# A new step list for a block-sparse attention and mixer kernel: engine order, load issues and PSUM banks

## The chip, the cores and the metric

The kernel runs on one core of a Trainium2 chip. The metric is the time of one execution on the device in microseconds (us); less is better. The time before is the median of 3 runs, 272.63 us (271.21 to 273.03).

## The reference, cut to what matters

Four batches, 8 heads, 768 positions, head size 64. Attention with a block mask (32 x 32 blocks: neighbours, the first and last block, and 3 sampled blocks for each block row), then a low-rank mix over the positions, then a two-layer network with a residual:

```python
scores = scale * np.matmul(q, k.transpose(0, 1, 3, 2))
scores = np.where(mask, scores, -1000000000.0)
attn = np.exp(scores - max); attn = attn / (sum + 1e-09)
x = np.matmul(attn, v)                      # heads side by side: (4, 768, 512)
u = x + (x.transpose(0, 2, 1) @ U @ V).transpose(0, 2, 1)      # rank 32
out = u + np.maximum(u @ w_ch1, 0.0) @ w_ch2                   # 512 -> 2048 -> 512
```

## The kernel before, in words

Tiles have 128 partitions. Heads are worked on in pairs, so there are 16 pairs, four to a batch: pairs 0 to 3 are batch 0, 4 to 7 batch 1, and so on. For each pair TensorE makes scores (keys by queries), ScalarE writes their exponential to the tile `est`, VectorE multiplies by the 0/1 `mask` (for pairs 0 to 3 the mask is added inside the score product instead, and no multiplication follows), and TensorE multiplies `est` with the values `vt`, with a column of ones for the row sums. VectorE then divides: `divide` (L538) is a reciprocal (L544) and one or two multiplications (L551). The mix goes through `Ut` and `Vt`; the result, transposed, is `uT`, for the products with the first weight `w1t` (`w1`, L679; matmuls L685) into PSUM, a rectifier into `hid` by ScalarE (L697) or VectorE (L699), and the products with the second weight `w2t` (`product`, L756, matmuls L760). The products with `w2t`, and for the last batch those with `w1t` too, are done as seven block products instead of eight (Strassen's scheme), which needs sums and differences of weight blocks (`weight_sum`, L723, VectorE, L721) and of token blocks.

PSUM has 8 banks. Every product is told its bank in the list; a product into a bank waits until the last reader of that bank is through.

The order is written out by hand: the string `PLAN` (L448) is a list of words, and a loop (L1141) issues each word's instructions to the engines in that order. Every engine works through its own instructions strictly in the order of the list and waits where an operand or a bank isn't ready; between engines only such waits order the work. So a word's place sets what stands ahead of it and behind it on its engine. The words that matter here:

- `S`, `B`: a score product of pairs 0 to 3, over one or two key tiles. `Q`: the scores of both heads of a pair over two key tiles (three `Q` make a pair; two `H` can stand for one `Q`). A digit is the bank.
- `e`: the exponential (ScalarE) of the oldest score product; `p`: the multiplication by the mask (VectorE), L1045.
- `A`, `V`: the products with the values; `v`: the division (VectorE) of the oldest finished one, two for each pair.
- `R`, `Z` without dots: transposes of q and k by TensorE; `t`, `z`: their copies out of PSUM (VectorE).
- `M`, `X`, `Y`, `E`, `m`, `y`, `g`: parts of the mix and their copies or sums.
- `P`, `C`, `U`: products with `w1t`; `P2` is the first half of one into bank 2, `P6` into bank 6; `a`, `b`: the rectifier on ScalarE or VectorE.
- `q.k.n`: weight sum k of half n. `S.`, `H.`, `D.`: sums, products and result sums of the down projection of batches 0 to 2; `g.`, `c.`, `o.`, `r.`, `s.`, `h.`, `e.`: the last batch.
- `F.`, `x.`, `d.`, `T.`: the mix at the end of a batch; `T.i` is the transpose of pair i's part to `uT` by a DMA (L623).
- `Z.b.tau.u`: a store of one row group of batch b (L707). `L.i`: loads: the DMA transposes of q and k of pair i + 2 (`front`, L386, SP queue) and the loads of pair i + 3 (GpSimd queue, L146).

The second weight comes in four loads on GpSimd's queue, each of four row tiles j of 16 (`load_w2`, L370), two of them among the loads of pair 7 and two among those of pair 8:

```python
for j in js:                                   # 0, 4, then 8, 12
    nc.gpsimd.dma_start(out=w2t[:, j : j + 4, :], in_=moe_w_ch2[j * P : (j + 4) * P, :]...)
```

A weight sum with k = 3 is `t1 = b12 - b11`, and for half n = 0 it reads row tiles 0 to 3 of `w2t`; k = 4 reads tiles 8 to 11 (n = 0) or 12 to 15 (n = 1):

```python
c, js = slice(n, n + 1), slice(n * NH // 2, (n + 1) * NH // 2)     # NH = 8
b11, b21 = w2t[:, 0:NH, 0:DM][:, js], w2t[:, NH:, 0:DM][:, js]
b12, b22 = w2t[:, 0:NH, DM:][:, js], w2t[:, NH:, DM:][:, js]
...
    3: (t1, b12, b11), 4: (t2, b22, t1), 5: (t4, b21, t2), ...
```

`t1` goes to the tile `res`, in which q and k of pairs 0 to 3 lay. It is an operand of product 5 of the down projection (`H.b.tau.5`).

Of the kernel before, what the change touches and what calls it, by code (L numbers as in the profile page):

```python
# [23 lines left out]
def kernel(  # L24
# [16 lines left out]
    B, H, S, D = q.shape  # L41
    BLK = 32
    NB = S // BLK
    T = S // P
# [404 lines left out]
    S0 S3 e e S5 B0 e Z7 e S3 z Z6 e z B0 A7 A e R6 S3 t A R5 e A B0 t A K6 e A S3 k v A5 A e K6 k B0 A  # L449
    A e K7 A K6 k S3 k A K7 e v B0 k S3 e M6 e A5 A m R7 A t B0 K6 R3 e k A A t S6 A e v S0 D2 S3 e d A7  # L450
    A e A S0 K6 A e S3 k K2 A e S5 k A e v S3 R2 e S5 t S0 e M7 e S3 m D2 e B5 d A0 D1 e A A d A S3 D2 A
    e d K1 S5 k R7 e S3 t A S1 e v A5 A e A S3 S6 e K2 A e A k A S3 v B0 e K7 M6 e k S3 m X5 K7 e A6 Y k
    A B0 y X7 Y e S3 y E5 A e A g A R7 S0 t A e v S4 S2 e A7 A e R1 E6 A t A g A A Q v e e M6 X7 m Y P6
    y p H U7 e p H b C e p H b U7 e p H b U6 e p E1 a g p V7 Q v e e V6 U7 v p U0 a P1 b C p P6 a C E7 Q
    a g U6 e e U7 b P6 b p U0 C a U7 p a Q b X6 Y e e P7 y C P6 b C p U0 b a p V7 L.5 Q v U.0.1.3.6 e
    q.3.0 V7 a.0.1.3.0 e U.0.1.1.1 v U.0.1.11.0 a.0.1.1.1 U.0.1.5.6 q.3.1 a.0.1.11.1 p Q a.0.1.5.1 p
    U.0.1.10.6 e U.0.1.7.7 a.0.1.10.0 e U.0.1.2.6 a.0.1.7.0 S.0.0.1.3 U.0.1.9.7 p a.0.1.2.1 Q a.0.1.9.1
    q.7.1 U.0.1.4.6 e S.0.0.2.0 H.0.0.1.0.7 p H.0.0.1.1 a.0.1.4.1 U.0.1.0.0 p L.6 e U.0.1.14.1 q.4.1 V6
    a.0.1.0.1 p a.0.1.14.1 Q v q.4.0 e V6 D.0.0.0 S.0.0.3 H.0.0.6.0 e v U.0.1.13.2 q.7.0 H.0.0.6.1
    U.0.1.12.6 a.0.1.13.1 D.0.0.2 y p Q a.0.1.12.1 q.5.1 H.0.0.7.0 e H.0.0.7.1 q.5.0 H.0.0.5.0.6 D.0.0.3  # L460
    H.0.0.5.1 e S.0.0.4.4 U.0.1.6.1 p H.0.0.4.0 a.0.1.6.1 H.0.0.4.1 D.0.0.4 Q D.0.0.5 p H.0.0.3.0 e L.7
    H.0.0.3.1 p H.0.0.2.0.7 H.0.0.2.1 e p U.0.1.8.2 U.0.1.15.0 D.0.0.1 D.0.0.6 a.0.1.8.1 V7 p a.0.1.15.1
    S.0.1.1.1 Q S.0.2.1.0 V6 e v S.0.1.2.4 H.0.1.1.0.7 y v H.0.1.1.1 y H.0.1.2.0.0 S.0.2.2.3 y H.0.1.2.1
    e D.0.1.0 M6 D.0.1.1 H.0.2.1.0.1 m H.0.2.1.1 S.0.2.3 F.1.0.2.4 D.0.2.0 F.1.1.3.6 F.1.2.5.0 x.6.0
    H.0.2.6.0 x.6.1 d.6.0 H.0.2.6.1 x.7.0 d.6.1 F.1.3.6.4 D.0.2.2 H.0.1.6.0 T.6 x.5.1 H.0.1.6.1 S.0.1.3
    H.0.2.7.0 H.0.2.7.1 x.4.0 H.0.2.5.0.6 x.5.0 H.0.2.2.0.0 D.0.2.3 d.5.0 H.0.2.2.1 x.4.1 d.5.1
    H.0.2.4.0 D.0.1.2 d.4.0 T.5 x.7.1 H.0.2.4.1 d.7.0 H.0.1.7.0 D.0.2.1 d.4.1 D.0.2.5 H.0.1.7.1 d.7.1
    S.0.2.4.2 T.4 Q D.0.1.3 H.0.2.5.1 e H.0.1.4.0 T.7 D.0.2.4 H.0.1.4.1 H.0.2.3.0 e D.0.1.5 H.0.2.3.1
    Z.0.0.1 p H.0.1.5.0.7 Z.0.2.1 H.0.1.5.1 D.0.2.6 Q Z.0.2.0 D.0.1.4 Z.0.0.0 S.0.1.4.0 U.1.0.0.6 e
    H.0.1.3.0 a.1.0.0.0 H.0.1.3.1 e U.1.0.11.6 D.0.1.6 p U.1.0.10.0 Z.0.1.0 Z.0.1.1 a.1.0.11.1 U.1.0.9.7  # L470
    p L.8 a.1.0.10.1 U.1.0.6.6 a.1.0.9.1 p Q a.1.0.6.1 p U.1.0.12.6 e V7 e U.1.0.2.2 v U.1.0.5.0 p
    a.1.0.12.1 U.1.0.1.7 a.1.0.5.1 a.1.0.2.1 U.1.0.3.6 a.1.0.1.0 p Q a.1.0.3.1 V6 p e U.1.0.4.7 v e
    U.1.1.5.2 a.1.0.4.0 U.1.0.15.6 p a.1.1.5.1 U.1.1.9.7 a.1.0.15.1 p Q a.1.1.9.1 U.1.1.3.7 e L.9
    U.1.0.7.6 a.1.1.3.0 e U.1.0.14.7 a.1.0.7.0 p U.1.1.4.0 U.1.1.10.6 a.1.0.14.1 a.1.1.4.0 U.1.1.1.7 p
    a.1.1.10.1 Q a.1.1.1.1 V7 e V6 v e U.1.1.7.7 v Q a.1.1.7.1 p U.1.0.8.7 e H.1.0.1.0.6 a.1.0.8.0
    H.1.0.1.1 p e U.1.1.13.7 p U.1.0.13.0 U.1.1.14.2 p a.1.0.13.1 a.1.1.13.1 U.1.1.8.3 S.1.0.1.3
    a.1.1.14.1 U.1.1.6.7 a.1.1.8.1 S.1.0.3 Q a.1.1.6.1 S.1.0.2.0 H.1.0.2.0.7 e D.1.0.0 L.10 H.1.0.2.1
    S.1.0.4.4 H.1.0.6.0 D.1.0.1 H.1.0.6.1 e U.1.1.15.1 U.1.1.11.0 a.1.1.15.0 U.1.1.0.7 p a.1.1.11.1 Q
    D.1.0.2 a.1.1.0.1 p y V7 e H.1.0.7.0 v e H.1.0.7.1 U.1.1.2.0 p U.1.1.12.7 D.1.0.3 a.1.1.2.1 p Q
    a.1.1.12.1 S.1.1.1.0 H.1.0.4.0 e H.1.0.4.1 S.1.1.2.1 V7 D.1.0.5 e S.1.1.3 H.1.1.1.0.6 p H.1.1.1.1 Q  # L480
    D.1.1.0 v H.1.1.6.0 e L.11 p H.1.1.6.1 H.1.0.5.0.7 D.1.1.2 H.1.0.5.1 e p H.1.1.7.0 H.1.1.7.1 D.1.0.4
    V0 y p y y H.1.1.5.0.3 S.1.1.4.3 y V4 y D.1.1.3 v H.1.1.5.1 v y H.1.1.4.0 H.1.1.4.1 S.1.2.1.1 y
    H.1.0.3.0 D.1.1.4 M4 S.1.2.2.0 H.1.0.3.1 m D.1.1.5 F.2.0.5.4 F.2.1.0.1 D.1.0.6 Z.1.1.1 H.1.2.1.0.6
    x.8.0 H.1.2.1.1 x.10.0 d.8.0 H.1.1.3.0 x.10.1 d.10.0 F.2.2.7.5 D.1.2.0 F.2.3.4.2 d.10.1 H.1.2.2.0.1
    x.8.1 T.10 H.1.2.2.1 x.11.0 H.1.1.3.1 x.9.0 d.11.0 H.1.2.6.0 x.11.1 d.8.1 H.1.2.6.1 d.9.0 D.1.1.6
    T.8 H.1.1.2.0.7 D.1.2.1 d.11.1 x.9.1 H.1.1.2.1 S.1.2.3 d.9.1 Q T.11 D.1.2.2 D.1.1.1 e H.1.2.7.0
    H.1.2.7.1 T.9 H.1.2.5.0.7 D.1.2.3 e H.1.2.5.1 S.1.2.4.2 H.1.2.4.0 Z.1.1.0 H.1.2.4.1 Z.1.0.1 Q
    D.1.2.5 D.1.2.4 U.2.0.4.6 p e H.1.2.3.0 a.2.0.4.0 H.1.2.3.1 e U.2.0.12.6 D.1.2.6 U.2.0.5.7 Z.1.2.0
    Z.1.0.0 a.2.0.12.1 Q Z.1.2.1 a.2.0.5.0 p U.2.0.2.7 e L.12 U.2.1.8.6 a.2.0.2.0 U.2.1.1.7 a.2.1.8.1 e
    U.2.0.11.2 a.2.1.1.0 U.2.0.15.6 p a.2.0.11.1 U.2.0.0.7 p Q a.2.0.0.1 p a.2.0.15.1 U.2.0.9.7 e V6  # L490
    a.2.0.9.0 p e U.2.0.8.0 v U.2.0.10.7 a.2.0.8.1 U.2.1.4.6 a.2.0.10.0 p Q a.2.1.4.1 V7 p e U.2.1.0.6 v
    e U.2.0.13.1 a.2.1.0.0 U.2.0.1.7 p a.2.0.13.1 U.2.1.2.6 a.2.0.1.1 p Q a.2.1.2.0 U.2.1.9.7 e L.13
    U.2.0.7.6 a.2.1.9.0 e U.2.0.6.7 a.2.0.7.0 p U.2.0.14.6 a.2.0.6.1 q.0.1 Q a.2.0.14.1 p V7 e q.0.0 V6
    v e q.1.1 U.2.0.3.7 v Q a.2.0.3.1 p H.2.0.1.0.7 e p U.2.1.5.6 H.2.0.1.1 S.2.0.1.4 e U.2.1.10.0
    a.2.1.5.0 U.2.1.14.1 S.2.0.2.1 a.2.1.10.0 U.2.1.3.6 a.2.1.14.1 D.2.0.0 Q S.2.0.3 a.2.1.3.1 p
    H.2.0.6.0 e H.2.0.2.0.6 p H.2.0.6.1 H.2.0.2.1 e D.2.0.2 U.2.1.13.0 D.2.0.1 S.2.0.4.3 H.2.0.7.0
    a.2.1.13.1 H.2.0.7.1 p y Q p V6 e D.2.0.3 H.2.0.4.0 v e H.2.0.4.1 V6 D.2.0.5 p Q v U.2.1.11.7 e
    H.2.0.5.0.6 a.2.1.11.0 H.2.0.5.1 q.1.0 e U.2.1.12.7 p U.2.1.15.0 p a.2.1.12.1 U.2.1.7.1 a.2.1.15.1
    U.2.1.6.7 p a.2.1.7.1 Q a.2.1.6.1 D.2.0.4 y S.2.1.1.4 Z.2.0.1 H.2.2.1.0.7 e H.2.2.1.1 S.2.1.3
    H.2.0.3.0 D.2.2.0 H.2.0.3.1 e p H.2.1.1.0.1 H.2.1.1.1 S.2.2.1.2 H.2.1.2.0.0 y V3 p y y S.2.1.2.3 y  # L500
    V4 v D.2.1.0 H.2.2.5.0.5 y v H.2.1.6.0 H.2.1.6.1 S.2.2.3 y H.2.1.2.1 S.2.2.2.1 M3 D.2.0.6 H.2.2.5.1
    m Z.2.0.0 D.2.1.2 F.3.0.6.3 F.3.1.4.2 x.12.0 H.2.2.6.0 x.12.1 H.2.2.6.1 d.12.0 H.2.1.7.0 x.14.0
    d.12.1 H.2.1.7.1 x.14.1 d.14.0 T.12 D.2.2.2 F.3.2.4.6 d.14.1 F.3.3.2.3 x.13.0 H.2.2.7.0 x.13.1
    H.2.2.7.1 d.13.0 T.14 H.2.1.5.0.4 x.15.0 d.13.1 H.2.2.2.0.2 x.15.1 d.15.0 H.2.2.2.1 D.2.2.3 d.15.1
    T.13 D.2.1.3 H.2.1.5.1 S.2.1.4.2 H.2.1.4.0 H.2.1.4.1 D.2.2.4 T.15 D.2.1.4 H.2.2.4.0 D.2.2.1
    H.2.2.4.1 S.2.2.4.3 H.2.1.3.0 D.2.1.5 H.2.1.3.1 D.2.2.5 Z.2.1.1 H.2.2.3.0 D.2.1.6 H.2.2.3.1 q.6.1
    g.5.1.7 t.1 g.3.1.3 c.5.1.2 g.0.1.2 D.2.2.6 c.3.1.3 g.1.1.6 t.2 g.5.2.4 c.1.1.0 t.3 g.2.1.1 g.3.6
    D.2.1.1 c.2.1.1 g.1.2.5 o.5.1 Z.2.1.0 c.3.2.5 g.5.6 o.1.1 Z.2.2.1 g.2.6 g.3.2.0 Z.2.2.0 q.6.0
# [675 lines left out]
```

## Time and profile before

| | before |
|---|---|
| median of 3 runs | 272.63 us (271.21 to 273.03) |
| the profiled execution's own time | 271.49 us |
| its span in the profile | 269.7 us |
| TensorE (PE) matmul busy | 263.0 us, 97% |
| VectorE (DVE) busy | 232.5 us, 86% |
| ScalarE (ACT) busy | 202.6 us, 75% |
| GpSimd (POOL) busy | 72.8 us, 27% |
| end of the last matmul | 266.5 us |

The span runs from the first instruction to the last in the profile; the time of the execution has some 1.8 us around it. A busy time is a union over the whole span. PE stands for the matmuls, PEld for the weight loads that overlap them, SP for the engine that only issues DMAs here. A matmul's record in the profile is longer than the step from one matmul to the next, since they are pipelined; work on a stretch is counted by those steps. L-numbers are lines of the kernel before; in the kernel after, lines behind the list are 3 less.

### The profile page before, as it was taken

How to read it: one execution, taken by the hardware profiler on the slowest of the kernel's cores; microseconds unless marked ns; L12 is line 12 of the kernel's file. 1: busy time of each engine (PE TensorE's matmuls, PEld its weight loads, DVE VectorE, ACT ScalarE, POOL GpSimd, SP SyncE). 2: the span in 40 equal slices, each digit the busy share in tenths (PEclk: the TensorE clock that was granted, in tenths of full speed). 3: DMA queues.
4: the chain of work that ended last, by engine and by line, in shares of the span. 5: the costliest groups of instructions: out<-in, count | busy, mean ns of one | idle time of the engine just before them, and what ended most of it. 6: DMA issues, size and time to landing. Idle time of an engine off the chain costs nothing.

```text
span 269.7 us, 7319 instructions
## 1 busy us (share of the span) xinstructions
PE 263.0 (97%) x3015; PEld 183.3 (68%) x3015; DVE 232.5 (86%) x476; ACT 202.6 (75%) x264; POOL 72.8 (27%) x100
## 2 busy tenths in 40 slices
PE   8899999999999999999999999999999999999995
PEld 4577776565567778665666888565667788666884
DVE  5699988988999998877588998678998999999993
ACT  4889998897989666789898857787997944789200
POOL 5469204955451760060707070000000000000000
PEclk9999999999999999999999999999999999999999
DMA  5799997999999999898949898620300115400024
GB/s 154 241 293 302 208 198 169 96 134 164 187 143 128 119 108 103 268 116 82 95 37 86 91 96 148 218 50 2 61 0 2 41 41 117 160 0 0 2 97 136
DMA packets 88720, 31.66 MB, mean 117 GB/s; under 512 B 77104, under 2 KB 85840, under 8 KB 88688
## 3 DMA queue, kind: packets, MB, share of 16 engines
q0 software_dynamic: 49728, 10.10, 49.5%
q1 hardware_dynamic: 38384, 20.68, 33.3%
q8 instruction: 23, 0.38, 0.6%
q10 hardware_dynamic: 576, 0.44, 0.5%
q14 instruction: 9, 0.07, 0.1%
HBM read 27.67 MB, written 6.29 MB: 126 GB/s over the span
## 4 chain that ended last, share of the span: by engine, by line
PE 63%; DMA 12%; DVE 6%; issue 2%; POOL 2%; ACT 1%; SPq 1%; DVEq 0%; POOLq 0%
PE ps L760 31%; PE ps L685 17%; DMA w2t<-in_moe_w_ch_dram 8%; PE ps L414 7%; PE ps L1030 7%; DMA vld<-in_v_dram 2%; DMA qpl<-stqld 2%; DVE est L1045 1%; ACT est L1039 1%; DMA uT<-xh 1%; PE ps L665 1%; DVE sums L721 1%; DVE xf L551 1%; POOL vt L146 1%; POOL stkld L146 1%
## 5 line engine op out<-in xcount | busy, mean ns | idle before, releaser
L1039 ACT ACTIVATE est<-ps 128x1536 f16<-128x1536 f32 x72 | 100.6, 1450 | 18.8 <-PE ps L1030 18.7
L685 PE MATMUL ps<-uT,w1t 128*128 128x384 f16 x384 | 70.4, 326 | 0.1
L1045 DVE TENSOR_TENSOR est<-est,mask 128x1440 f16<-128x1440 f16 x72 | 63.4, 903 | 0.6 <-ACT est L1039 0.2
L685 PEld LDWEIGHTS <-w1t 128*128 128x128 f16 x384 | 35.5, 97 | 26.6 <-issue 6.8
L414 PEld LDWEIGHTS <-est 128*128 128x128 f16 x1152 | 40.5, 97 | 7.3 <-issue 3.2
L414 PE MATMUL ps<-vt,est 128*128 128x65 f16 x1152 | 43.3, 193 | 0.5 <-DVE xf L551 0.5
L760 PEld LDWEIGHTS <-hid 128*128 128x128 f16 x358 | 33.9, 98 | 6.7 <-issue 1.6
L697 ACT ACTIVATE hid<-ps 128x384 f16<-128x384 f32 x63 | 29.8, 495 | 5.1 <-PE ps L685 4.7
L1030 PE MATMUL ps<-qpl,kpl 64*128 64x512 f16 (+1 forms) x288 | 31.7, 325 | 0.0
L146 POOL DMA_DIRECT2D stqld<-in_q_dram x20 | 16.3, 820 | 55.3 <-DMA qpl<-stqld 54.7
L760 PE MATMUL ps<-w2t,hid 128*128 128x256 f16 x238 | 31.1, 273 | 0.0
L879 DVE TENSOR_TENSOR xf<-xf,ps 128x256 f32<-128x256 f32 x63 | 25.5, 418 | 4.5 <-PE ps L760 3.7
L699 DVE TENSOR_SCALAR hid<-ps 128x384 f16<-128x384 f32 x33 | 18.3, 555 | 9.0 <-PE ps L685 8.2
L760 PEld LDWEIGHTS <-sums 128*128 128x128 f16 x216 | 20.2, 98 | 4.8 <-issue 1.0
L989 ACT ACTIVATE est<-ps 128x768 f16<-128x768 f32 x30 | 22.5, 813 | 0.6 <-PE ps L980 0.6
L1030 PEld LDWEIGHTS <-kpl 64*128 64x128 f16 x288 | 12.3, 94 | 14.2 <-issue 9.1
L760 PE MATMUL ps<-res,sums 128*128 128x256 f16 x144 | 19.4, 273 | 0.2 <-DVE xf L879 0.2
L634 ACT CAST xh<-xf 128x384 f16<-128x384 f32 x24 | 11.0, 510 | 10.4 <-DVE xf L630 10.4
L551 DVE TENSOR_TENSOR xf<-ps,rcp 128x384 f32<-128x384 f32 x32 | 17.7, 554 | 0.8
L146 POOL DMA_DIRECT2D vt<-in_v_dram x20 | 16.3, 820 | 2.3 <-DMA vt<-in_v_dram 2.2
L146 POOL DMA_DIRECT2D stkld<-in_k_dram x20 | 16.3, 819 | 2.3 <-DMA kpl<-stkld 1.6
L760 PE MATMUL ps<-res,hid 128*128 128x256 f16 x120 | 15.9, 273 | 0.0
(122 smaller groups left out, 341.4 us busy)
## 6 DMA issues: line engine op xcount, KB each, us to landing
out_dram<-xf SPq DMA_DIRECT2D x18, 256.0 KB, 2.3
vld<-in_v_dram SPq DMA_DIRECT2D x6, 384.0 KB, 5.2
w1t<-in_moe_w_ch_dram POOLq DMA_DIRECT2D x4, 512.0 KB, 8.1
w2t<-in_moe_w_ch_dram POOLq DMA_DIRECT2D x4, 512.0 KB, 11.1
qld<-in_q_dram SPq DMA_DIRECT2D x5, 384.0 KB
kld<-in_k_dram SPq DMA_DIRECT2D x5, 384.0 KB, 5.9
stqld<-in_q_dram POOLq DMA_DIRECT2D x20, 96.0 KB, 4.4
stkld<-in_k_dram POOLq DMA_DIRECT2D x20, 96.0 KB, 4.2
```

The costliest lines, as they stand in the source:

```text
L146: nc.gpsimd.dma_start(out=dst[:, h], in_=src[b, 2 * hp + h].rearrange("(p t) d -> p t d", t=T),)
L414: nc.tensor.matmul(pav[:, sc, :], est[:, n, sc * P : (sc + 1) * P], vts[b % 2][:, 2 * hp + h, g, 0 : D + 1], start=(g == 0 and sc == 0), s ...
L551: nc.vector.tensor_tensor(out=dst, in0=pav[:, :, 0:D], in1=rcp[:, :, None].broadcast_to([P, T, D]), op=ALU.mult,)
L685: nc.tensor.matmul(pt, w1t[:, cc, jj * P : (jj + 1) * P], bts[b].uT[:, cc, c * HS : (c + 1) * HS], start=(cc == 0), stop=(cc == NCC - 1), ...
L697: nc.scalar.activation(out=dst, in_=pt, func=AF.Relu)
L699: nc.vector.tensor_scalar_max(out=dst, in0=pt, scalar1=0.0)
L760: nc.tensor.matmul(acc[key], lhsT, rhs, start=(first and i == 0), stop=(i == len(pairs_) - 1), skip_group_check=True,)
L879: nc.vector.tensor_add(out=x, in0=x, in1=acc[a, b, tau])
L989: lambda: nc.scalar.activation(out=dst, in_=ps, func=AF.Exp, scale=0.125),
L1030: nc.tensor.matmul(units[h][:, u * S + lo : u * S + hi], kT[drows[h], g * P : (g + 1) * P], qT[drows[h], lo:hi], start=True, stop=True, sk ...
L1039: nc.scalar.activation(out=both[h], in_=units[h].rearrange("p (g n) -> p g n", g=2), func=AF.Exp, scale=0.125,)
L1045: lambda: nc.vector.tensor_mul(out=masked(both[h]), in0=masked(both[h]), in1=masked(mask[:, 2 * j : 2 * j + 2, :]),),
```

## The change

The string `PLAN` is replaced by another; nothing else differs. The new list has the same 1278 words as kinds and counts go, with the same division of the rectifiers between ScalarE and VectorE; it differs in the order and in the banks. Some stretches that the text speaks of, cut:

```diff
     PLAN = """
-    S0 S3 e e S5 B0 e Z7 e S3 z Z6 e z B0 A7 A e R6 S3 t A R5 e A B0 t A K6 e A S3 k v A5 A e K6 k B0 A
+    S0 e S3 Z7 z S5 e e B1 Z0 z S4 e e A6 A A B0 e S3 e R5 t R7 t A A A v B0 S3 e e K7 A5 A A B0 e K6 K3 K4
...
     (from the first scores of pair 4 to those of pair 6)
-    Q v e e M6 X7 m Y P6 y p H U7 e p H b C e p H b U7 e p H b U6 e p E1 a g p V7
-    Q v e e V6 U7 v p U0 a P1 b C p P6 a C E7
-    Q a g U6 e e U7 b P6 b p U0 C a U7 p a
-    Q b X6 Y e e P7 y C P6 b C p U0 b a p V7 L.5
-    Q v U.0.1.3.6 e q.3.0 V7 a.0.1.3.0 e U.0.1.1.1 v U.0.1.11.0 a.0.1.1.1 U.0.1.5.6 q.3.1 a.0.1.11.1 p
+    Q M6 m X7 Y y P6 e p e p H U7 b H C b e e p p H e U7 b p H e U6 a E0 g V7
+    Q e e p V6 v q.3.0 v U7 U0 E1 g P2 P6 C C a b a a p p
+    Q e e U6 U7 b P6 U1 b a C a U7 p p
+    Q e e b X6 Y y P7 C b p P6 C b U1 a p V7 v
+    Q e e S.0.0.1.3 S.0.0.2.0 q.3.1 U.0.1.3.6 a.0.1.3.0 V7 v q.4.0 S.0.0.3 U.0.1.11.0 a.0.1.11.1 ...
...
     (pair 7's last scores, where L.7 stood)
-    Q D.0.0.5 p H.0.0.3.0 e L.7 H.0.0.3.1 p H.0.0.2.0.7 ...
+    Q e e H.0.0.3.1 H.0.0.3.0 D.0.0.6 H.0.0.2.0.7 ...
...
     (end of batch 1's mix, to the scores of pair 9)
-    ... T.6 ... T.5 ... T.4 Q D.0.1.3 H.0.2.5.1 e H.0.1.4.0 T.7 ... Z.0.0.1 p ... Z.0.2.1 ...
-    Q Z.0.2.0 D.0.1.4 Z.0.0.0 ... Z.0.1.0 Z.0.1.1 ... L.8 ...
+    ... T.7 ... T.5 Z.0.0.0 F.1.0.2.3 x.6.0 x.4.0 d.4.0 T.4 x.6.1 d.6.1 d.6.0 T.6 ...
+    Q e e p H.0.2.5.1 ... D.0.2.6 Z.0.2.0 H.0.1.5.0.7 ...
+    Q e e p U.1.0.0.6 ... U.1.0.6.7 a.1.0.6.1 L.7
+    Q e e U.1.0.12.6 a.1.0.12.1 p p V7 ...
...
     (the end)
-    h.2.4.3 e.2.5 h.1.4.2 h.1.4.3 e.1.5 h.2.3.1 h.2.3.2 h.2.3.3.8 e.2.6.0 e.2.6.1
+    h.2.4.3 e.0.6 h.2.3.2 h.2.3.0 h.2.4.0 h.2.4.1 e.2.5 h.2.3.3.8 h.2.3.1 e.2.6.1 e.2.6.0
     """
```

## The prediction

> **What bounds the kernel now.** I read the page first, then busy time by stretch, the chain that ended last, and then VectorE, TensorE, GpSimd and the SP queue in order of time. The page's first row:
>
> ```profile
> PE 263.0 (97%) x3015; PEld 183.3 (68%) x3015; DVE 232.5 (86%) x476; ACT 202.6 (75%) x264; POOL 72.8 (27%) x100
> ```
>
> TensorE is busy 263.0 of 269.7 us. Of the 6.7 us that are left, 0.8 lie ahead of the first matmul and 3.2 behind the last one (it ends at 266.5), so 2.7 us of visible pauses are all that a better order could give back, and any pause that a new order adds is added to the span. VectorE is the second bound: by stretch it is busy 18.05 of 20 us between 50 and 70, and 36.97 of 40 between 70 and 110. Whatever holds VectorE there soon holds TensorE, because TensorE writes its next product into a PSUM bank that VectorE must have read.
>
> The chain that ended last crosses, between 50 and 76 us, the loads of the second weight `w2t`, four loads of 512 KB:
>
> ```profile
> 49.76 1.62 POOL vt L146 x2
> 51.38 9.49 DMA w2t<-in_moe_w_ch_dram
> 60.87 0.28 issue
> 61.15 0.75 POOL w2t L372
> 61.91 2.27 issue
> 64.18 0.01 POOLq L146
> 64.19 11.19 DMA w2t<-in_moe_w_ch_dram
> 75.38 0.03 issue
> ```
>
> The first column is the start, the second the length. The first quarter of `w2t` (rows j 0 to 3) is issued at 51.38 and has landed at 60.87; the second has landed by 64.2, the fourth by 75.38, the third between. VectorE in the same time, and its first use of `w2t`:
>
> ```profile
> 53.24 0.19 DVE L544 RECIPROCAL rcp<-ps 128x6 f32<-128x6 f32 x1
> 53.46 0.56 DVE L551 TENSOR_TENSOR xh<-ps,rcp 128x384 f16<-128x384 f32 x1
> 53.93 0.55 DVE L551 TENSOR_TENSOR xf<-ps,rcp 128x384 f32<-128x384 f32 x1
> 54.88 0.20 DVE L544 RECIPROCAL rcp<-ps 128x6 f32<-128x6 f32 x1 [0.40 <-PE ps L414]
> 55.11 0.56 DVE L551 TENSOR_TENSOR xh<-ps,rcp 128x384 f16<-128x384 f32 x1
> 55.59 0.55 DVE L551 TENSOR_TENSOR xf<-ps,rcp 128x384 f32<-128x384 f32 x1
> ...
> 67.48 0.68 DVE L721 TENSOR_TENSOR res<-w2t 128x1024 f16<-128x1024 f16 x1
> ```
>
> The two groups of three are the two `v` steps (one for each head of pair 4) and the last line is `q.3.0`, the difference of two parts of the first quarter. In the list before, `q.3.0` comes 6.6 us after the landing, so nobody waits.
>
> **The change, part by part.** The list keeps every step: the same words with the same counts, 3015 matmuls, 476 VectorE, 264 ScalarE and 100 GpSimd instructions. The load order of GpSimd's queue is unchanged. So the sum is one of waits alone.
>
> *Part 1: `q.3.0` moves from pair 6 to pair 5, between the two `v` steps of pair 4.* VectorE gets to it when the first `v` is through: 53.93 + 0.47 (the step from one such instruction to the next) = 54.4. It reads `w2t` rows 0 to 3, which land at 60.87; nothing in the new list makes that load earlier, since the GpSimd queue and what stands ahead of it (transposes of pair 5, the loads of pair 6) are the same. So VectorE stands from 54.4 to 60.9. Its result is wanted only in product 5 of the batch-0 down projection, some 25 us later. Queued behind it are the second `v`, `g`, two `b` and two `p`.
>
> Who waits: TensorE at the same time is
>
> ```profile
> 52.75 0.82 PE L1030 MATMUL ps<-qpl,kpl 64*128 64x512 f16 x8
> 53.51 1.27 PE L414 MATMUL ps<-vt,est 128*128 128x65 f16 x36
> 54.62 2.76 PE L685 MATMUL ps<-uT,w1t 128*128 128x384 f16 x16
> ```
>
> In the new list the second value product `V6` (36 matmuls from 53.51) is followed by `U7 U0 E1 P2` and then `P6`. At 163 ns for each 384-column matmul, `U7 U0` take 8 x 0.163 = 1.30, `E1` 3 x 0.056 = 0.17, `P2` 2 x 0.163 = 0.33, so TensorE reaches `P6` at 54.6 + 1.8 = 56.4. `P6` writes bank 6, which holds the result of `V6` until the second `v` has read it. That `v` now runs after `q.3.0`: 60.95 + 0.60 + 0.23 + 0.47 + 0.55 = 62.8. TensorE stands from 56.4 to 62.8: **6.4 us**. It isn't won back: TensorE has no spare time later, and VectorE, at over 90% in the next 50 us, stood for as long. As a lower bound: if the quarter landed as soon after its issue as the 96 KB loads of v beside it (median 4.6 us), at 56.0, the pause would be 56.1 + 0.60 + 0.23 + 0.47 + 0.55 - 56.4 = 1.5 us. As an upper one: with the 11.19 us of the fourth quarter it would be 8.1. I take the load's own row, 9.49, since the traffic around it is the same.
>
> *Part 2: the pace of TensorE after the pause.* The trace shows no pause over 0.8 us, except the time before the first matmul. There it begins like this:
>
> ```profile
> 0.79 4.32 PE L278 MATMUL ps<-const-bfloat16-1.0 128*128 128x512 bf16 x15 [0.79 <-PEq L1168]
> ```
>
> These are 8 matmuls of 512 columns and 7 of 128, 4992 columns, and the next group starts at 5.04: 4992 / 4.25 us = 1.17 columns per ns, where sixteen L685 matmuls later take 2.60 us, 2.36 columns per ns. So after a long rest TensorE ran at half pace for 4.25 us and lost 2.1 us (the row of the granted clock says 9 tenths or more throughout, so I read it from the spacing). Short pauses of up to 0.7 us cost nothing of the kind: L685 and L414 keep their spacing behind them. A pause of 6.4 us lies between; the bounds are 0 and 2.1. I take 2.1, because a pause of many matmuls is more like the start than like a hiccup of half a microsecond.
>
> [...]
>
> *Part 3: the first scores.* The list before has two early waits of TensorE, 0.52 us at 8.26 and 0.72 us at 10.95, for VectorE's copies of head 1 (L293, L359). The new list turns head 1's q ahead of the third score and puts the copies `z` earlier, and three value products ahead of head 1's first pair of scores. That can give 1.2 us at most; but ScalarE is busy 18.80 of 20 us from 10 to 30, and sets the pace there. Bounds 0 and -1.2; I take -0.6.
>
> *Part 4: the SP queue at the turn of batch 1.* A store `Z` now stands between the four transposes of `uT`, another ahead of pair 9's two transposes (`L.7`), which used to be issued ahead of pair 8's scores.
>
> ```profile
> 100.68 8.59 SPq L623 DMA_TRANSPOSE uT<-xh  x4
> 109.38 3.97 SPq L707 DMA_DIRECT2D out_dram<-xf  x6
> 113.52 1.27 SPq L388 DMA_TRANSPOSE qpl<-stqld  x1
> 114.89 1.22 SPq L388 DMA_TRANSPOSE kpl<-stkld  x1
> ```
>
> A store takes 3.97 / 6 = 0.66 us of the queue, a transpose 1.3, and lands 1.6 after it. On the clock of before, the second store's sums are done at about 109.3; so 109.3 + 0.7 + 2 x 1.3 + 1.6 = 114.2 for pair 9's transposes, where TensorE starts pair 9 at 114.56. It fits with 0.3 us to spare. Cost 0; if VectorE is later in that stretch the transposes are too, up to 2 us as a bound.
>
> *Part 5: all other moves* (PSUM banks, the grouping of `e` and `p`, the last phase). The same work stands on each engine between the same score blocks, give or take a few steps. Bounds: -1.5 (what is left of the 2.7 us of pauses) and +1.5 (as much again). I take 0. At the end two half-width sums of 0.29 us each follow the last matmul as before.
>
> Sum by the span: 269.7 + 6.4 + 2.1 - 0.6 = 277.6. The profiled execution took 271.49 with a span of 269.7, 1.8 more; the median of the runs, 272.63, is 1.1 above it. So the median after is 277.6 + 1.8 + 1.1 = **280.5 us**.
>
> **Rivals.**
>
> *Half pace doesn't come* (the pause leaves TensorE at full pace): 280.5 - 2.1 = 278.4. For it: no row shows the pace falling within the run. Against it: the start. Chance 0.25.
>
> *Pair 9's transposes come late on top of it*: 280.5 + 2 = 282.5. For it: only 0.3 us to spare. Against it: after the pause the DMA queues are emptier than before. Chance 0.08.
>
> *On the other side: the first quarter of `w2t` is there when `q.3.0` wants it.* Then part 1 and 2 fall away and 269.7 - 0.6 + 2.9 = 272.0 remains, no slower than before; with all of part 5's gain 270.5. It decides at 54.4 us: the load would have to land 3 us after its issue at 51.38, or VectorE reach `q.3.0` 6.5 us later than the rows say. The 96 KB loads beside it take a median of 4.2 to 4.6 us for a fifth of the bytes; the row of the load itself shows 9.49. Chance 0.12.
>
> **How the numbers follow.** Forecast 0.55, and 0.25, 0.08, 0.12 as above. A measurement here tells about 1% (2.7 us) from no change. The first three cases, 0.88 together, are all slower by over 1%; the last is split into 0.05 for faster by over 1% (it needs part 5's gain too) and 0.07 for within 1%. The range goes from 275.5 (full pace, with part 5's gain and all of part 3's) to 283.5 (late transposes and 1 us of part 5's loss); it leaves out the last rival and a little above.
>
> **What would show it.** In the profile after: a VectorE instruction `res<-w2t` at about 61 us with some 6 us idle ahead of it, put down to the `w2t` DMA; a TensorE pause of about 6 us ending near 63 and put down to VectorE's L551 or its new line; and behind it 384-column matmuls spaced about 0.33 us for some 4 us. No such spacing means that part 2 is wrong. If `res<-w2t` comes at about 55 without a wait, part 1 is wrong and so is the forecast. A second pause near 120 us ahead of pair 9's scores, put down to `qpl` or `kpl`, would show part 4 wrong.

## The result, and the profile after

The kernel after takes 281.07 us (median of 6 runs, 279.64 to 283.8), the kernel before 272.5 (median of 6, 271.21 to 273.03): a ratio of 1.033, 95% interval 1.0287 to 1.0373. The forecast was 280.5, range 275.5 to 283.5. The profiled execution took 283.8 us, with a span of 282.0; it is the slowest of the six, which matters for the sizes below.

From the page of the kernel after, the busy row, TensorE's row and the row of the granted clock (40 slices of 7.05 us, in tenths):

```profile
PE 266.3 (94%) x3015; PEld 183.0 (65%) x3015; DVE 231.8 (82%) x476; ACT 202.2 (72%) x264; POOL 72.7 (26%) x100
...
PE   8999999907999999999999999799999999999995
...
PEclk9999999985999999999999999999999999999999
```

The instruction counts are the same. TensorE is idle through the ninth slice and part of the tenth, and there the clock row, which before showed only nines, falls to 8 and 5. A second, smaller dent stands in slice 26.

VectorE of the kernel after, in order of time, around the place (start, length, line, operation, and in brackets the idle time ahead and what ended it; lines behind the list are 3 less than before):

```profile
54.20 0.55 DVE L548 TENSOR_TENSOR xf<-ps,rcp 128x384 f32<-128x384 f32 x1
63.55 0.69 DVE L718 TENSOR_TENSOR res<-w2t 128x1024 f16<-128x1024 f16 x1 [8.79 <-DMA w2t<-in_moe_w_ch_dram]
64.16 0.19 DVE L541 RECIPROCAL rcp<-ps 128x6 f32<-128x6 f32 x1
...
64.85 0.55 DVE L548 TENSOR_TENSOR xf<-ps,rcp 128x384 f32<-128x384 f32 x1
```

`q.3.0` stands between the two `v` steps and waits 8.79 us for the first quarter of `w2t`. The chain that ended last goes through that load, which took 12.64 us here instead of 9.49:

```profile
50.88 12.64 DMA w2t<-in_moe_w_ch_dram
63.52 0.02 issue
63.55 0.04 DVE res L718
```

TensorE in the same stretch, and its waits over the whole span (total, times, longest):

```profile
56.30 0.49 PE L682 MATMUL ps<-uT,w1t 128*128 128x384 f16 x2
65.45 2.08 PE L682 MATMUL ps<-uT,w1t 128*128 128x384 f16 x6 [8.67 <-DVE xf L548]
```

```profile
PE ps L682 <- DVE xf L548: 8.7, 1, 8.7
PE ps L682 <- DMA uT<-xh: 1.6, 1, 1.6
```

The last product ahead of the pause is `P2` at 56.30, the first behind it `P6`, which starts as the second `v` ends. That is the place and the cause that the forecast named. The second wait, at 182.6 us, it did not name.

Behind the pause the clock is at 0.50. Busy time by stretch (us, then busy time of PE, PEld, DVE, ACT and POOL, then the granted clock, the DMA share and GB/s), with edges set on the clock's own changes:

```profile
57.42:60.83 3.41, 0.00 (x0) 0.00 (x0) 0.00 (x0) 0.00 (x0) 0.34 (x1) 1.00 0.93 132
60.83:64.24 3.41, 0.00 (x0) 0.00 (x0) 0.69 (x2) 0.00 (x0) 0.91 (x2) 0.50 1.40 171
64.24:67.66 3.42, 2.21 (x8) 0.84 (x9) 3.39 (x7) 0.58 (x2) 1.06 (x2) 0.50 3.47 98
67.66:71.07 3.41, 3.41 (x15) 1.34 (x12) 0.86 (x2) 2.51 (x3) 2.88 (x4) 0.50 2.23 162
71.07:74.50 3.43, 3.43 (x27) 1.87 (x26) 2.66 (x4) 1.85 (x4) 2.00 (x3) 1.00 1.24 207
```

The clock falls at 60.83 and is back at 71.07, 10.24 us later. TensorE works from 65.45 on, so 5.62 us of work are done at half pace (384-column matmuls 320 ns apart instead of 163) and 2.8 us are lost.

Where the time went, by the start of the same score product in the two traces (after minus before): +0.2 us at the scores of pair 4; +11.5 behind the pause and the half clock; +10.6 through pairs 9 to 11; +12.2 from pair 12's third scores on; +12.0 at pair 15's scores and +12.2 at the last matmul. Values in between shift a little with the work that the list moves across a score block. So 8.7 of pause and 2.8 of pace are 11.5 of the 12.3 us of span. The other moves gave back 1.0 us up to pair 9, and the 1.6 us at the turn of batch 2 (in front of pair 12's third scores) took more than that.

### The profile page after: what moved, and what is told of

Its sections match the earlier page's. It is cut to its first block, busy times and chain, and to the rows that moved or that the text cites. A ratio compares the mean times of both kernels' runs of the same rounds, so it can differ in the third digit from the quotient of the medians.

```text
span 282.0 us, 7324 instructions
## 1 busy us (share of the span) xinstructions
PE 266.3 (94%) x3015; PEld 183.0 (65%) x3015; DVE 231.8 (82%) x476; ACT 202.2 (72%) x264; POOL 72.7 (26%) x100
## 4 chain that ended last, share of the span: by engine, by line
PE 78%; DMA 9%; DVE 7%; POOL 2%; issue 1%; ACT 1%; SPq 0%; DVEq 0%; POOLq 0%
PE ps L757 31%; PE ps L682 22%; PE ps L414 9%; PE ps L1027 8%; DMA w2t<-in_moe_w_ch_dram 4%; PE ps L977 2%; DMA vld<-in_v_dram 2%; DMA uT<-xh 2%; PE ps L278 2%; DVE res L966 1%; PE ps L996 1%; DMA qpl<-stqld 1%; DVE xf L548 1%; PE ps L662 1%; DVE res L293 1%
## 5 line engine op out<-in xcount | busy, mean ns | idle before, releaser
L682 PE MATMUL ps<-uT,w1t 128*128 128x384 f16 x384 | 72.4, 333 | 10.3 <-DVE xf L548 8.7
L682 PEld LDWEIGHTS <-w1t 128*128 128x128 f16 x384 | 36.1, 99 | 36.8 <-issue 17.7
L414 PEld LDWEIGHTS <-est 128*128 128x128 f16 x1152 | 38.8, 97 | 6.2 <-issue 4.0
L414 PE MATMUL ps<-vt,est 128*128 128x65 f16 x1152 | 41.3, 193 | 0.0
L146 POOL DMA_DIRECT2D stqld<-in_q_dram x20 | 16.3, 820 | 63.5 <-DMA qpl<-stqld 62.9
```

The costliest lines, as they stand in the source:

```text
L146: nc.gpsimd.dma_start(out=dst[:, h], in_=src[b, 2 * hp + h].rearrange("(p t) d -> p t d", t=T),)
L414: nc.tensor.matmul(pav[:, sc, :], est[:, n, sc * P : (sc + 1) * P], vts[b % 2][:, 2 * hp + h, g, 0 : D + 1], start=(g == 0 and sc == 0), s ...
L682: nc.tensor.matmul(pt, w1t[:, cc, jj * P : (jj + 1) * P], bts[b].uT[:, cc, c * HS : (c + 1) * HS], start=(cc == 0), stop=(cc == NCC - 1), ...
```

## The experiments

The time at half clock in one execution, worked out as 2 x (1 - mean granted clock) x span, is given where it says something; up to 1.3 us of it lies behind the last matmul, where the clock falls as well (in the trace of the run with N = 14 below, from 282.09 to the end of the span at 283.36). The mean clock is recorded in thousandths, so each such time is good to some 0.3 us.

### The word moved back

```diff
-    Q e e p V6 v q.3.0 v U7 U0 E1 g P2 P6 ...
+    Q e e p V6 v v U7 U0 E1 g P2 P6 ...
...
-    Q e e S.0.0.1.3 S.0.0.2.0 q.3.1 ...
+    Q e e S.0.0.1.3 S.0.0.2.0 q.3.0 q.3.1 ...
```

> The new list with one word moved: q.3.0 goes from between the two v steps of pair 4 back to pair 6, just ahead of q.3.1; all else is the new list. Theory A (the forecast: the wait for the first quarter of w2t, and the half pace behind it, are the whole loss): the pause of 8.7 us at P6 goes, and with it the stretch of 0.320 us matmuls (36 of them at 0.32 instead of 0.163 cost 2.8 us), so a span of 282.0 - 8.8 - 2.8 = 270.4 and a time of about 272.2, within 1% of before. The granted clock is 1.00 throughout. Rival B (the rest of the list costs as much: banks, stores, transposes): TensorE pauses elsewhere and the time stays above 276. A middle result is also possible: the 1.6 us pause that the profile after shows at 182.6, in front of the products with uT of batch 2, stays.

Measured: 273.41 us (12 runs, 272.05 to 276.57), ratio to before 1.0041 (1.0011 to 1.007); clock 1.00 in the profiled execution. The longest of the twelve, 276.57, had 3.3 us at half clock; there is no trace of it. TensorE's waits, and two lines of VectorE and TensorE in order of time:

```profile
PE ps L682 <- DMA uT<-xh: 1.3, 1, 1.3
PE ps L682 <- DVE hid L696: 1.3, 2, 0.9
```

```profile
73.09 0.69 DVE L718 TENSOR_TENSOR res<-w2t,res 128x1024 f16<-128x1024 f16 x1 [0.94 <-DMA w2t<-in_moe_w_ch_dram]
74.91 1.30 PE L682 MATMUL ps<-uT,w1t 128*128 128x384 f16 x7 [0.88 <-DVE hid L696]
```

One word out of 1278 accounts for 7.7 of the 8.6 us by the medians. The pause for `uT` stays, and two small ones appear for rectifiers. The first (0.44 us at 71.05) stands behind the two weight sums that now follow one another. The second and longer one (0.88 us at 74.91) stands behind `q.4.0`, which waits 0.94 us for the third quarter of `w2t`: the new list has a second weight sum that can come ahead of its data. Theory A stands, with a rest of about 1 us. (The 2.8 us of pace that the expectation takes off is half of the 5.62 us of work at half clock; only 13, not 36, of the 384-column matmuls start there.)

### The word alone moved ahead in the list before

```diff
-    Q v e e V6 U7 v p U0 a P1 ...
+    Q v e e V6 q.3.0 U7 v p U0 a P1 ...
...
-    Q v U.0.1.3.6 e q.3.0 V7 a.0.1.3.0 ...
+    Q v U.0.1.3.6 e V7 a.0.1.3.0 ...
```

> The list before with one word moved: q.3.0 goes from pair 6 ahead to pair 5, behind V6 and so between the two v steps of pair 4, as in the new list; all else is the list before. Theory A: VectorE waits for the first quarter from about 54.5 until it lands (60.9 to 63.5), TensorE pauses at the next product into bank 6 from about 57.3 on for 5.6 to 8.1 us, then runs some 5.6 us at half pace (2.8 us lost): 269.7 + 5.6 to 8.1 + 2.8 = 278.1 to 280.6 of span, 280 to 283 us of time. Rival B (the loss comes from other parts of the new list, and the list before has room for the wait): less than 274.

Measured: 279.17 us (278.27 to 281.9), ratio 1.0274 (1.0225 to 1.0322). VectorE's wait and TensorE's:

```profile
61.75 0.69 DVE L721 TENSOR_TENSOR res<-w2t 128x1024 f16<-128x1024 f16 x1 [7.14 <-DMA w2t<-in_moe_w_ch_dram]
```

```profile
63.66 1.44 PE L685 MATMUL ps<-uT,w1t 128*128 128x384 f16 x4 [6.80 <-DVE xf L551]
```

The word by itself is enough: the kernel before with this one edit loses 7 us, by the same two lines. The median is 0.8 us below the range expected for theory A and well above the rival's 274. Three of the four executions had only 3.3 or 6.7 us at half clock; the profiled one, 281.9, had 10.24 in its trace. This trace, of the old list but for the one word, also has a wait of 1.00 us for `uT` at the turn of batch 2 (at 180.44).

### TensorE kept busy through the pause

In `w1`, for the first half of the product that stands as `P2` only:

```diff
-        for cc in ccs:
+        again = 22 if (b, c, jj, ccs[0]) == (0, 0, 1, 0) else 0
+        for cc in list(ccs) * (1 + again):
```

> The new list as it is, but the two matmuls of P2 (pair 5), the last ones ahead of the pause, are issued 23 times instead of once, each time into the same bank with the same result: 44 matmuls more, 44 x 0.163 = 7.2 us of work in the place of the pause. Theory A (a rest of TensorE sets its clock to half): the wait itself stays as long, at most 1.7 us of it is left as a pause, or the repeats run past its end by up to 1 us; the granted clock stays at 1.00 and the 2.8 us of half pace are saved: some 278 us, and no matmuls 0.32 us apart behind it. Rival B (the half pace comes from something else at that time, such as the traffic of w2t or VectorE's restart): clock 0.5 and spacing 0.32 stay, and the time is 281 or more.

Measured: 279.04 us (278.82 to 279.73). TensorE and, below, two stretches of the same execution:

```profile
55.91 8.61 PE L683 MATMUL ps<-uT,w1t 128*128 128x384 f16 x52
```

```profile
58.00:62.00 4.00, 4.00 (x27) 2.43 (x25) 2.12 (x5) 0.00 (x0) 0.75 (x1) 1.00 1.25 182
62.00:66.00 4.00, 4.00 (x29) 2.10 (x28) 2.27 (x4) 1.56 (x3) 2.56 (x4) 1.00 2.96 142
```

VectorE waits for the quarter as before (5.49 us, until 59.85 here), but the clock stays at 1.00. The repeats ran 1.7 us past the end of the second `v` (61.71), more than the 1 us that was allowed for; the time is 1 us above the expected 278, and still 2 us below the kernel after. VectorE's stop and restart and the load of `w2t` were there as before, only TensorE's rest was not, and the half pace did not come (clock 1.00 in both stretches): here it came with the rest.

### The word later, a shorter pause

```diff
-    Q e e p V6 v q.3.0 v U7 U0 E1 g P2 P6 C C a b a a p p Q e e U6 U7 ...
+    Q e e p V6 v v U7 U0 E1 g P2 P6 C C a b a a p p q.3.0 Q e e U6 U7 ...
```

> The new list with q.3.0 moved 13 words back, behind the second p of pair 5's first scores; VectorE comes to it at about 58.5 and waits for the quarter until 61 to 63.5, and TensorE, which has work until about 60, pauses for 2.1 to 4.6 us at a product whose bank VectorE has to free. In the profile after, the granted clock fell 4.1 us after the last matmul (56.7 to 60.8). Theory A (the clock falls only when TensorE has rested for about 4 us): no half pace unless the pause is over 4 us, so 270.4 + 2.1 to 4.6 = 272.5 to 275.0 of span and 274.3 to 276.8 of time, clock 1.00. Rival B (every pause of over 1 us costs the half pace): the same pause and 2 to 3 us more, clock below 0.99.

Measured: 274.46 us (9 runs, 273.16 to 277.17), ratio 1.0115 (1.0075 to 1.0155). The profiled execution (273.28) had the pause of the first line; the second is the stretch around it between two points of the grid of 3.41 us on which the changes of the clock lie, a window in what follows (the last section has the measurements):

```profile
61.23 2.11 PE L682 MATMUL ps<-uT,w1t 128*128 128x384 f16 x12 [1.55 <-DVE hid L696]
```

```profile
59.38:62.79 3.41, 1.86 (x12) 1.04 (x11) 2.78 (x5) 2.10 (x4) 0.75 (x1) 1.00 1.41 168
```

The pause is shorter than the 2.1 us at least that were expected, as the quarter had landed at 59.99, early for this load. Two groups: five executions of 273.2 to 274.5 us with at most 0.5 us at half clock, four of 275.7 to 277.2 with 3.3 to 3.9. A pause of 1.55 us cost no pace, so rival B falls. The four slower executions lost pace; that their pauses were longer is likely, but there is no trace of them. (The word moves by 15 places here, not 13.)

### The load earlier, the list as it is

```diff
-        if i in (HP, HP + 1):
-            load_w2(range((i - HP) * NJJ // 2, (i - HP + 1) * NJJ // 2, 4))
+        if i in (HP - 2, HP + 1):
+            load_w2(range(0, NJJ // 2, 4) if i < HP else range(NJJ // 2, NJJ, 4))
```

> The new list unchanged, with q.3.0 still between the two v steps; but the first two quarters of w2t are issued by GpSimd behind the loads of pair 4, at about 29 us, where its queue is empty until 41 us, instead of at 51 us. Theory A (the loss is the wait for the transfer, not the place of the word as such): the quarter has landed long before 54.5, VectorE and TensorE do not wait, no half pace: the same as with the word moved back, 282.0 - 8.8 - 2.8 = 270.4 of span, or up to 1.5 more with the pause for uT at the turn of batch 2: 272 to 274 us. Rival B (1 MB more between 29 and 41 us, 5 us of traffic at the 200 GB/s of that stretch, delays the loads of q, k and v of pairs 4 and 5): a pause of 1 to 3 us of TensorE appears between 35 and 50 us, 274 to 276 us.

(By the code, the first two quarters stand behind the loads of pair 6 in the kernel before and the last two behind those of pair 7, one pair earlier than the words ahead of the prediction have it; the edit moves the first two to behind the loads of pair 4.)

Measured: 273.67 us (12 runs, 272.76 to 279.06), ratio 1.0045 (1.0017 to 1.0072). `q.3.0` runs at 56.57 with no idle time ahead of it, so it was the transfer that counted. But the earlier traffic has a price: from the list's first score product to pair 5's first scores this execution takes 47.88 us, where six traces of the new list with the loads in their old place take 45.75 to 45.77 (five) and 46.34. Part of it is a wait for `uT` (0.66 us at 47.05); 1.09 us more at the turn of batch 2 is the wait that the list had anyway. Two of the twelve executions took 278.3 and 279.1, with 10 us at half clock; no trace of those two exists. Both theories hold in part: the wait for the quarter goes, the earlier traffic costs, and the median is level with that of the word moved back (273.41).

### The turn of batch 2

On top of the first experiment:

```diff
-    ... d.8.1 H.1.1.3.0 H.1.2.1.0.6 H.1.2.1.1 x.10.1 d.10.1 d.10.0 T.10 T.8 ...
+    ... d.8.1 T.8 H.1.1.3.0 H.1.2.1.0.6 H.1.2.1.1 x.10.1 d.10.1 d.10.0 T.10 ...
-    Q e e U.2.0.4.6 a.2.0.4.0 H.1.2.3.1 H.1.2.3.0 D.1.2.6 q.0.1 U.2.0.12.6 ...
+    Q e e H.1.2.3.1 U.2.0.4.6 a.2.0.4.0 H.1.2.3.0 D.1.2.6 q.0.1 U.2.0.12.2 ...
```

> sum_back (the new list with q.3.0 back in pair 6) and, at the turn of batch 2, T.8 issued five steps earlier, right behind d.8.1, one block of eight matmuls (H.1.2.3.1) ahead of the first product with the new uT (U.2.0.4) instead of behind it, and U.2.0.12 in bank 2 instead of 6. sum_back has a pause of 1.3 us there, put down to the transposes of uT. Theory A (the four transposes, 1.3 us each on SP's queue, end too late for the first product): T.8 earlier gives 0.9 us and the eight matmuls 0.87 us of cover, the pause goes, 273.4 - 1.3 = 272.1 us, level with the kernel before. Rival B (the transposes are late because of the traffic, whatever stands on the queue): the pause stays and so does 273.4.

Measured: 272.16 us (12 runs), ratio 1.0012 (0.9984 to 1.004). No wait for `uT` is left. The four transposes on the SP queue begin at 162.72 instead of 164.31; 0.7 of these 1.6 us is the whole execution being earlier (pair 12's second scores start at 169.18 and 169.84), so the edit gives 0.9. By the medians the time is 1.25 us less than with the word moved back alone, which is what was expected; the two intervals overlap. `H.1.2.3.1` is four matmuls in the trace and covers 0.44 us, not eight and 0.87. The edit changes three things at once, so which of them ended the wait isn't shown.

Nor is the queue the whole of the wait. In the kernel after, the last of the four transposes ends the wait:

```profile
177.90 4.62 DMA uT<-xh
```

Against pair 12's second scores it is issued only 0.5 us later than in the kernel before (166.84 there, scores 10.54 us earlier), but it takes 4.62 us to land, where the `uT` transposes of the kernel before have a median of 2.8. So the slower landing is the larger part. Its cause stays open, and rival B can't be ruled out: the earlier issue may only have made room for it.

### Two versions without either pause

`both` is the early load with the edit of the turn, `q.3.0` in its new place; `place_turn` has the loads as they were, the edit of the turn, no `q.3.0` between the two `v`, and

```diff
-    Q e e b X6 Y y P7 C b p P6 C b U1 a p V7 v ...
+    Q e e b X6 q.3.0 Y y P7 C b p P6 C b U1 a p V7 v ...
```

> The early load of w2t (as in early_load) and the edit at the turn of batch 2 (as in turn), with q.3.0 in its new place. If both theories hold, neither pause is left: 270.4 + 1.8 = 272.2, less the 1.3 of the transposes = 270.9 to 271.5 us, up to 0.5% faster than the kernel before. If the early load costs traffic, 273 or more.

> The edit at the turn of batch 2 (as in turn), the loads of w2t as they were, and q.3.0 in pair 5 ahead of the last Y, where VectorE comes to it at about 64 us: later than the quarter lands (60 to 63.5), and with room behind it, while in pair 6 it stood together with q.3.1 ahead of a rectifier for which TensorE waited 0.9 us. Theory A: no pause for w2t and the 0.9 us of the rectifier saved against turn: 271.2 to 272 us. Rival B (the place is too near to the landing): in some executions a wait of up to 1 us, and 272 to 273.

Measured: `both` 272.59 us (ratio 1.001, 0.9985 to 1.0034), `place_turn` 271.99 (0.9989, 0.9958 to 1.002). Neither can be told from the kernel before. `both` missed its expectation by more than 1 us and came out 0.4 below its rival's 273. The early load's traffic is seen to cost again: from the list's first score product to pair 5's first scores the profiled execution takes 46.69 us, 0.9 more than with the loads in their old place. `place_turn` fell into its range; it ran `q.3.0` at 62.29 with no wait in its profile. The 0.9 us of the rectifier that it was to save was not there to be had: the profile of `turn` has 0.4 us for it, that of `place_turn` 0.53, and the 0.88 of the word moved back stood behind `q.4.0`. One of its twelve executions took 274.85.

### Pauses of a set length

On top of `both`, where the quarter is there in time:

```diff
+            for _ in range(N if (k, n) == (3, 0) else 1):      # N = 6, 9, 14
                 minus(v, *{ ...
```

> both (early load, turn of batch 2 mended), with the one instruction of q.3.0 issued 6 times in a row, each time with the same result. One step is 0.60 us, so VectorE reaches the second v 3.0 us later, and TensorE, which in both gets to P6 as that v ends, pauses for 3.0 us, in every execution alike. In the executions so far the time at half clock, worked out from the mean granted clock as 2 x (1 - clock) x span, was near 0, 3.3, 6.7 or 10.2 us, so multiples of 3.4. Theory A (the clock is set at the ends of windows of 3.4 us that run freely, and falls after a window with no work): a pause of 3.0 us never holds such a window; clock 1.00 in every execution and 272.6 + 3.0 = 275.6 us. Rival B (it falls after any pause of 2 to 3 us): clock 0.98 to 0.99, 277 to 279.

> As hold6, with 9 issues: a pause of 8 x 0.60 = 4.8 us. Theory A: a pause of 4.8 us holds a whole window of 3.4 us in (4.8 - 3.4) / 3.4 = 4 of 10 executions; in the others the clock stays 1.00 and the time is 277.4; in those it falls, with 3.4 or 6.8 us at half clock in all, and 1.7 to 3.4 us are lost: 279 to 281. So two groups of times. Rival B (the clock falls a fixed 4.1 us after the last matmul and comes back a fixed 5.6 us after the first, as in the profile after): all executions alike, 0.7 + 5.6 = 6.3 us at half clock, 277.4 + 2.8 = 280.2.

> As hold6, with 14 issues: a pause of 13 x 0.60 = 7.8 us. Theory A: it always holds a window; 6.8 or 10.2 us at half clock in all, of which those behind the pause cost half: 272.6 + 7.8 + 1.7 to 3.4 = 282.1 to 283.8, in two groups by the share of the windows. Rival B: all alike, 3.7 + 5.6 = 9.3 us at half clock, 283.2.

| | pause in the profile | time, us | at half clock in each execution, us |
|---|---|---|---|
| N = 6 | 2.98 | 278.72 (277.88 to 282.04) | 3.9, 3.9, 7.8, 14.0 |
| N = 9 | 5.61 | 281.11 (278.61 to 281.54) | 6.6, 6.7, 6.7, 7.8 |
| N = 14 | 9.24 | 284.53 (283.98 to 285.5) | 10.1, 10.2, 10.2, 11.3 |

The pauses for N = 9 and 14 are longer than expected because one repeat took 0.72 us (9 in 6.48), not 0.60. The first expectation failed: in the profiled execution a pause of 2.98 us lowered the clock. The three executions without a trace lost one or two windows too; their pause is estimated at 3.4 to 3.5 us (the 5.61 of N = 9 less three repeats), since in the profiled one TensorE came to the place late, after the half clock told of below. The profile of N = 6 by windows of 3.41 us, laid on the changes of its clock at 47.80, 58.04, 64.87 and 68.28:

```profile
44.39:47.80 3.41, 2.05 (x15) 0.79 (x12) 2.70 (x5) 2.51 (x2) 0.00 (x0) 1.00 1.03 168
...
61.46:64.87 3.41, 1.08 (x9) 0.59 (x8) 3.27 (x6) 1.34 (x2) 2.55 (x4) 1.00 2.06 135
64.87:68.28 3.41, 2.76 (x12) 1.12 (x13) 3.16 (x6) 0.98 (x2) 1.63 (x2) 0.50 2.17 160
68.28:71.70 3.42, 3.42 (x24) 1.78 (x21) 2.06 (x4) 2.96 (x3) 2.54 (x4) 1.00 1.25 206
```

The clock fell at 64.87 behind a window in which TensorE was busy for 1.08 of 3.41 us, and was back behind one of 2.76. So the window ahead of the fall was not empty, and theory A as worded fails here. With N = 9 all four executions fell. By itself this says little: for a pause of 5.61 us theory A as worded gives 6 or 7 of 10, not the 4 of 10 that were put down for 4.8. In its profile the clock stayed low behind a window of 1.13 us:

```profile
62.23:65.64 3.41, 1.13 (x4) 0.55 (x4) 3.34 (x8) 0.00 (x0) 3.41 (x5) 0.50 2.34 154
65.64:69.06 3.42, 3.42 (x15) 1.18 (x14) 1.38 (x2) 2.03 (x3) 3.35 (x5) 0.50 1.51 198
```

Rival B, with fixed delays, doesn't fit either, though it had N = 6 and the likeness of the executions right: the clock fell 3.3 us after the last matmul with N = 9 and 5.1 us with N = 14, and came back 4.5 and 6.1 us after the first. N = 14 is 0.7 us over its range, with a pause 1.4 us longer than was put in.

In N = 6 the clock had fallen once before, at 47.80, behind a wait of 1.27 us for `uT`, and stayed at 0.50 for three windows (10.24 us) though TensorE was busy throughout. Busy time doesn't explain that case: the first two of the three windows were full (3.41 and 3.42 us) and the clock stayed at 0.50 behind both. With N = 9 and 14 the wait at the same place was 0.81 and 0.80 us, and the four 384-column matmuls behind it took 0.82 us, in N = 6 1.46. What kept the clock low in N = 6 isn't shown, and no run was made for it. The two executions with the early load and 10 us at half clock may be the same case.

## Why the prediction came out as it did

*Part 1 (the wait for the first quarter): right in place and cause, short in size for the profiled execution.* Taking the word back removes 7.7 us, and the word alone in the old list costs 7. The pause was put at 6.4 us, bounds 1.5 to 8.1; it measured 8.67 in the profiled execution, above the upper bound, and 6.80 in the old list with the word moved. The term that was mis-sized is the load: "9.49, since the traffic around it is the same". In eight traces with the loads in their old place the quarter took 8.8 to 12.6 us, landing at 59.8 to 63.5. So 9.49 is a typical value (the median of the eight is 9.4), and the profiled execution has the longest of them. That spread is also the likeliest reason why six runs of the kernel after scatter over 4 us where six of before scattered over 2, though only one of the six has a trace: every microsecond of the load now stands on the path, and it decides between two windows and three at half clock.

*Part 2 (half pace): right, and proved apart from the pause by keeping TensorE busy.* It was put at 2.1 us, also its upper bound, from the start of the run; in the profiled execution it cost 2.8, since 5.62 us of work fell into the low windows, not 4.25. The start gave the size for its own case only: from the first matmul behind the pause to the rise of the clock it was 5.62 us here, 4.55 with N = 9 and 6.13 with N = 14, and half of that is lost. In four of the six executions the time at half clock was 6.7 to 7.3 us instead of 10.2; these took 279.64 to 281.19, and the median (between 280.96 and 281.19) is theirs. The rival without half pace (278.4, chance 0.25) fell with this.

*Part 3 (first scores, -0.6): right in sign, too large.* At pair 4's first scores the kernel after is 0.2 us later in the profile, but it was 0.46 later already at the list's first score product (7.21 against 6.75), ahead of which the two kernels are alike: the half pace of the start lasted to 6.21 us there and to 5.16 before. Counted from that product, pair 4's first scores come after 36.61 us in the two traces of the old list and after 36.36 to 36.38 in five of the new one with the loads in their place, so the list gives 0.24. The old waits of 0.52 and 0.72 us shrank, but a new one of 0.5 us ends at 15.2 (a transposed copy of q or k, put ahead of a mask product that needs its bank). I had looked only at the waits of the old list, not for new ones in the new.

*Part 4 (SP queue): right where it looked, and it looked at the wrong batch.* Pair 9's transposes were issued at 120.68 and 122.06; with 1.22 us each and 1.6 to land, the second is there at 124.9, and pair 9's scores started at 125.14 without a wait. The 0.3 us to spare held, and that rival fell. At the turn of batch 2 a wait for transposes did cost 1.6 us. The first product that reads `uT` stands right behind pair 12's second scores in both lists; the last transpose was issued 0.5 us later than before, and landed in 4.62 us instead of some 2.8. The forecast never walked through that turn, and with its "1.6 after it" for the landing it would have found only the smaller part.

*Part 5 (all else at 0): within its bounds.* With the word moved back the rest of the new list costs 0.4% (1.1 us, by the interval 0.3 to 1.9), where parts 3 to 5 had it at -0.6. The wait at that turn measures 1.3 there; with it gone nothing is left that can be told from the kernel before.

*The rival of a quarter that is there in time* (chance 0.12) fell: the earliest landing seen with the loads in their place is 59.8, five microseconds after VectorE asked.

That the sum came within 0.6 us of the median is partly luck: against the profiled execution it was 4.4 us short (2.3 of pause, 0.7 of pace, 0.8 up to pair 4's scores, more than half of that from the start of the run, 1.6 of the turn, less 1.0 that the other moves gave back). The median execution had less time at half clock, and probably shorter waits. The 1.1 us that the sum adds because the profiled execution of before lay below its median had the opposite sign after: there the profiled execution lies 2.7 above the median. The lower end of the range, 275.5, doesn't follow from the terms named for it, which give 280.5 - 2.1 - 1.5 - 0.6 = 276.3; nothing hung on it.

## What to carry to other kernels

In a kernel whose engines work in order, look in a new order first for an instruction that reads a freshly loaded tile: one cheap instruction placed ahead of its data (0.69 us here) holds up everything queued behind it (VectorE for 8.79 us, and TensorE for 8.67), whoever needs that. Size such a wait by the spread of the load's time (8.8 to 12.6 us here) and not by one row of it, and add what TensorE loses in pace after the pause (2.8 us here). When a wait is found at one turn of a loop, walk through every other turn of the same kind before giving the rest of the change a zero.

## What the runs showed of the hardware

All that follows is read from the traces and runs of this case. Every stretch at half clock within the work was 3.41, 6.83 or 10.24 us long, so one, two or three times 3.41: 10.24 in the kernel after (60.83 to 71.07), in the old list with the word moved (59.25 to 69.49) and with N = 14 (63.64 to 73.88), 6.83 with N = 9 (62.23 to 69.06), 10.24 and 3.41 with N = 6 (47.80 to 58.04, 64.87 to 68.28). The changes of the clock in one trace lie such steps apart also where the clock is full between them: in the kernel after it rises at 6.21 and falls at 60.83, 16 steps later, and with N = 6 it rises at 58.04 and falls again at 64.87, two steps later. So these traces can be divided into windows of 3.41 us from one change on. The executions without a trace agree (near 0, 3.3, 6.7 or 10.2 us by their mean clock, plus at most 1.3 behind the last matmul). So what a pause cost in pace came in steps, of up to 1.7 us (half of 3.41) for each such window of work, 2.8 us in the kernel after. The clock fell behind windows without work (0.00 us in the kernel after and with N = 14), and behind windows with 1.03 (old list with the word moved) and 1.08 us (N = 6) of work in 3.41 too.

Three windows behind which the clock fell or stayed, from the trace of the old list with the word moved (it fell to one half), that of N = 14 and that of the kernel after (both stayed):

```profile
55.83:59.25 3.42, 1.03 (x7) 0.49 (x5) 0.00 (x0) 1.55 (x3) 0.97 (x2) 1.00 1.44 94
```

```profile
56.81:60.23 3.42, 1.69 (x13) 0.95 (x11) 3.25 (x6) 1.85 (x3) 3.42 (x6) 1.00 1.88 122
```

```profile
180.29:183.71 3.42, 1.78 (x15) 1.25 (x14) 0.63 (x2) 2.79 (x2) 0.00 (x0) 1.00 0.01 1
```

The last one holds the wait of 1.6 us for `uT`, which therefore cost no pace. Windows at full clock, by the work that TensorE had in them: behind 0.00 (kernel after, N = 14), 0.08 (N = 9), 1.03 (old list with the word moved) and 1.08 us (N = 6) the clock fell; behind 1.69 (N = 14), 1.78 (kernel after) and 1.86 us (the word later) it stayed; behind the 2.05 us of N = 6 it fell. That last one is unexplained, as above.

In these traces the pace did not come back with the first matmul, nor always with the first window that had some work. Windows at half clock in which TensorE was busy for 1.13 (N = 9), 2.21 (kernel after), 2.42 (old list with the word moved) and 2.72 us (N = 14) were followed by another at half clock, one of 2.76 (N = 6) was not, but two of 3.41 and 3.42 (N = 6, from 47.80 on) were. Each was seen once.

The start of the run is at half pace too, in the kernels before and after, though the granted clock reads 1.00 there. Their traces show why: the first clock entry is the rise, at 5.16 us before and at 6.21 after, and the row counts what lies ahead of it as full. The spacing agrees: in the kernel after, matmuls of 128 columns start 0.107 us apart at 5.05 to 5.6 us and 0.056 apart from 6.3 on. So in these traces the pace ahead of the first entry has to be read from the spacing.
